# Linear attention with a gated convolution behind it: token-major products of queries with kv for the first two batches

## The chip, the cores and the metric

The kernel runs on one core of a Trainium2 chip. The metric is the device time of one execution in microseconds (us). A profiled execution gives the trace from which all durations here are read; its time differs a little from the median of the runs.

## The reference

For 8 batches and 8 heads, queries, keys and values have 576 tokens of 64 numbers. Features and attention, and then a gated feed forward on the 512 columns of all heads:

```python
proj = x @ w_phi                                  # 64 -> 128
proj = proj - max(abs(proj), axis=-1)
phi  = concat([exp(proj), exp(-proj)])            # 256 features
kv   = phi(k).T @ v                               # per batch and head, 256 x 64
z    = sum(phi(k), tokens)
x    = (phi(q) @ kv) / (phi(q) @ z + 1e-6)        # 576 x 64 per head
h    = relu(x @ w_in)                             # 512 -> 1024
c    = conv over 3 tokens of h with conv_w        # per column
out  = (h * sigmoid(c)) @ w_out                   # 1024 -> 512
```

The feed forward's weights come as float64 and are converted on the chip.

## The kernel before

**Units and groups.** A unit u = 2*batch + quad holds four heads as two pairs (pair index i). Its tokens go in five groups g: g = 0 is the last 64 tokens (both pairs in one group, n = 1), g = 1 to 4 are 256 tokens (n = 2) of two pairs in turn. `k_process` (L220) loads keys, projects them (`kp`, L185 ff.), subtracts the maximum (km L204, ks L206 on DVE), takes the exponentials `ke` on ACT (L236, L237) and multiplies them into `kv` (L251 for g = 0, L255 otherwise: weights are `ke`, 128 tokens by 128 features, f32; moving are 65 or 130 columns of v with a column of ones for the denominator). `q_process` (L300) projects queries, transposes them to features on partitions (`tp`, L320), takes exponentials (L326, `qe` or `qh`), and multiplies with kv to `nm` (L348 in f32, L356 in three fp32r terms of high and low halves): 65 rows, of which one is the denominator, and up to 256 token columns.

**Pairing.** Up to the first five groups of keys, a group's kv products are issued by `k_process` itself. Every later one hands its products over as a generator, and the nm products of the group five places earlier issue them alternately with their own (L331, L350 to L360; an nm, then one or two kv).

**Division.** ACT copies the denominator row (`dr`, L374), a DMA collects it into `den` (L377), ACT copies the numerator (`num`, L379). When two groups of a pair are there, `x_process` (L384) adds 1e-6 and takes the reciprocal on DVE (L392, L393), spreads it by four DMAs (`rr`, L397), broadcasts it with a stream shuffle (L405), multiplies (L406) and splits x into `xh` (ACT, L60) and `xl` (DVE, L65), for two halves c of the tokens.

**Feed forward.** `h_part` (L418) of batch b and half c multiplies x of all four pairs p with w_in in three fp32r terms (`hp`, L429), for eight column blocks; it needs x of every pair. Then relu, the convolution (POOL L452, DVE L457), sigmoid, gate, splits, and `op` with w_out (L488). The weights arrive in 16 chunks w0 to w15 (8 of w_in, then 8 of w_out) through two raw buffers and are converted by DVE (L96, L98, L100, L103), ACT (L97, L102, L60) and POOL (L105, L65).

**Order.** A planner (L513 to L586) steps these processes as generators with an own clock and ready times, and the instructions get priorities from the moment they were issued; each engine's order is fixed when the kernel is built. PE, DVE, ACT and POOL execute theirs strictly in that order. PSUM tiles of kp, qp, tp and nm share four buffers of a pool (`pg`, tag "g").

**Which units use f32.** NKV_F32 = 2: units 0 and 1 keep kv and the query features in f32 (`kvh` copied by ACT L282); later ones are split into high and low halves (kvf, kvh, kvl; ql on DVE L65).

Of the kernel before, what the change touches and what calls it, by code (L numbers as in the profile page):

```python
# [7 lines left out]
F32 = mybir.dt.float32  # L8
F32R = mybir.dt.float32r
# [19 lines left out]
AHEAD = 300  # L29

NQ_F32 = 2
NKV_F32 = 2


@with_exitstack
def kernel(
# [13 lines left out]
    nc = tc.nc  # L50
    cp = ctx.enter_context(tc.tile_pool(name="cp", bufs=1))
    sb = ctx.enter_context(tc.tile_pool(name="sb", bufs=1))
    pg = ctx.enter_context(tc.tile_pool(name="pg", bufs=4, space=bass.MemoryType.PSUM))
# [3 lines left out]
    def split(src, hi, lo, eng_hi, eng_lo):  # L57

        if eng_hi is nc.scalar:
            nc.scalar.activation(out=hi, in_=src, func=AF.Copy)  # L60
        elif eng_hi is nc.gpsimd:
            nc.gpsimd.tensor_scalar(out=hi, in0=src, scalar1=1.0, scalar2=0.0, op0=ALU.mult, op1=ALU.add)  # L62
        else:
            nc.vector.tensor_copy(out=hi, in_=src)
        eng_lo.tensor_tensor(out=lo, in0=src, in1=hi.bitcast(F32), op=ALU.subtract)  # L65
# [13 lines left out]
    idn = load_const(ident, [P, P], "idn")  # L79
# [73 lines left out]
    def pe(ns):  # L153
        return ("pe", ns)
# [61 lines left out]
    kv = {}  # L216
# [3 lines left out]
    def k_process(b, qd, g):  # L220
        j = (b * NQ + qd) * 5 + g
# [5 lines left out]
        n, hi, lo = load_split(kT, b, qd, g, "k")  # L227
# [6 lines left out]
        pr = project(n, hi, lo, b, qd, g, "k")  # L234
# [22 lines left out]
                                             start=False, stop=(g % 2 == 0 and t == 1), skip_group_check=True)  # L257
                        yield ins

        if j < 5:  # L260
            for _ in products():
                pass
            yield pe(860 * n)
        else:


            kvgen[j] = products()
            set_ready(("ke", j))
            yield until(("kvd", j))
        if g == 4:  # L270
# [3 lines left out]
            r = []  # L274
# [23 lines left out]
    xh, xl = {}, {}  # L298

    def q_process(b, qd, g):  # L300
        j = (b * NQ + qd) * 5 + g

        def back(key, k):
            return (key, *divmod(j - k, 5)) if j >= k else None

        yield until(back("qp", 2))
        n, hi, lo = load_split(qT, b, qd, g, "q")
# [3 lines left out]
        pr = project(n, hi, lo, b, qd, g, "q")  # L311
# [10 lines left out]
        qh = sb.tile([P, 2, 2, n * P], F32 if f32 else F32R, name=f"qh{b}_{qd}_{g}", tag="qh", bufs=2)  # L322
# [5 lines left out]
                split(e, qh[:, s], ql[:, s], nc.scalar, nc.vector)  # L328
        yield pe(220 * n)
        yield wait(3000)  # L330
        paired = j + 5 < 5 * NQ * B  # L331
        yield until(back("num", 1), ("kvq", b, qd), ("ke", j + 5) if paired else None)

        parts = [(0, 0, 512, 64), (1, 64, 512, 64)] if g == 0 else [((g - 1) // 2, 0, (g - 1) % 2 * 256, 256)]
        for pr_, _, _, _ in parts:
# [2 lines left out]
        ps = pg.tile([VW, 2, n * P], F32, name=f"nm{b}_{qd}_{g}", tag="g", bufs=4)  # L338
        ins = None
        for pr_, o, s0, w in parts:  # L340
            for i in range(2):
                khi, klo, kf = kv[b, qd][i]
                k = 0
                for s in range(2):
                    c_ = slice(pr_ * VW, (pr_ + 1) * VW)
                    a, x = (kf if f32 else khi)[:, s, c_], qh[:, s, i, o : o + w]
                    if f32:
                        ins = after(ins, lambda: nc.tensor.matmul(out=ps[:, i, o : o + w], lhsT=a, rhs=x,  # L348
                                                                  start=(s == 0), stop=(s == 1)))
# [17 lines left out]
        for pr_, o, s0, w in parts:  # L367
# [3 lines left out]
            dn, nt = den[b, qd, pr_], numt[b, qd, pr_]  # L371
# [9 lines left out]
        if g == 2 or g == 4:  # L381
            spawn(x_process(b, qd * 2 + g // 2 - 1))

    def x_process(b, p):  # L384
        yield ("wait", 4000)
        qd, pr = divmod(p, 2)
        dn, nt = den[b, qd, pr], numt[b, qd, pr]
        if 4 * b + p > 0:
            yield until(("x", *divmod(4 * b + p - 1, 4), 1))
        with tc.high_priority():  # L390
            rc = sb.tile([72, 16], F32, name=f"rc{b}_{p}", tag="rc", bufs=2)
            nc.vector.tensor_scalar(out=dn, in0=dn, scalar1=1e-6, scalar2=None, op0=ALU.add)  # L392
            nc.vector.reciprocal(out=rc, in_=dn)  # L393
            for i in range(2):
                for j in range(2):
                    row = D * i + 32 * j
                    nc.sync.dma_start(out=rr[row : row + 1, :].rearrange("o (r c) -> o r c", c=16),  # L397
                                      in_=rc.rearrange("(r i) c -> i r c", i=2)[i])
        yield ("wait", 4500)
        for c in range(2):  # L400
            yield until(("h", 2 * (b - 1) + c) if b > 0 else None)
            t0 = 0 if c == 0 else S - HW
            with tc.high_priority():
                xf = sb.tile([P, HW], F32, name=f"xf{b}_{p}_{c}", tag="xf", bufs=2)
                nc.vector.stream_shuffle(out=xf, in_=rr[:, t0 : t0 + HW], mask=[0] * 32)  # L405
                nc.vector.tensor_tensor(out=xf, in0=nt[:, t0 : t0 + HW], in1=xf, op=ALU.mult)  # L406
                xh[b, p, c] = sb.tile([P, HW], F32R, name=f"xh{b}_{p}_{c}", tag="xh", bufs=8)
                xl[b, p, c] = sb.tile([P, HW], F32R, name=f"xl{b}_{p}_{c}", tag="xl", bufs=8)
                split(xf, xh[b, p, c], xl[b, p, c], nc.scalar, nc.vector)
            set_ready(("x", b, p, c), 2500)  # L410
            yield pe(125)
# [117 lines left out]
    start = {}  # L529
# [113 lines left out]
```

## Time and profile before

| | |
|---|---|
| runs (us) | 824.35, 826.24, 827.76; median 826.24 |
| profiled execution (us) | 825.6, of which the span of the trace 823.5 |
| PE busy | 788.0 us (96%) |
| DVE busy | 645.6 us (78%) |
| ACT busy | 569.5 us (69%) |
| POOL busy | 307.6 us (37%) |

The span is from the first to the last instruction. An f32 matmul stands in the trace as two records; a PE row such as "x4" counts records. Matmuls are pipelined, so one record lasts about 0.28 us while the next can start 0.11 us after it; a price is therefore taken from starts. The granted clock (PEclk) is 1.00 at 2.4 GHz and 0.50 at 1.2 GHz.

### The profile page before, as it was taken

Reading aid. Unit: us, or ns where it says so; the run is one execution under the profiler, and the core shown is the slowest. Engines: PE = TensorE matmul, PEld = TensorE weight load, DVE = VectorE, ACT = ScalarE, POOL = GpSimd, SP = SyncE. Lnnn points to the kernel's source line nnn. Section 1 sums busy time; section 2 is a strip of 40 time slices with the busy share of each in tenths; the row PEclk is TensorE's granted clock in tenths of the full one; section 3 lists DMA queues with packets and bytes.
Section 4 is the critical chain, followed back from the end, with each engine's and each line's share of the span. In section 5 each row is a group of like instructions: output and inputs, shape, how many; then the busy total and the mean of one; then the engine's idle time right before and its main releaser. Section 6 shows DMA issues by size and latency. Waiting matters only on the chain.

```text
span 823.5 us, 17817 instructions
## 1 busy us (share of the span) xinstructions
PE 788.0 (96%) x6350; PEld 772.5 (94%) x6350; DVE 645.6 (78%) x1390; ACT 569.5 (69%) x1228; POOL 307.6 (37%) x467
## 2 busy tenths in 40 slices
PE   7778779999999999999999999999999999999998
PEld 6767678999999999999999999999999999999998
DVE  4879999799987769787779878788697878766551
ACT  4598777797788867687586857678576867644332
POOL 4757765444443424414233333424334131111110
PEclk9799989999999999999999999999999999999999
DMA  6544421211211302121121211112021100000001
GB/s 187 157 134 135 135 66 47 67 41 44 70 56 44 93 18 71 27 82 50 46 61 43 69 34 60 47 50 82 15 77 29 56 12 19 13 30 30 23 23 44
DMA packets 56328, 49.18 MB, mean 60 GB/s; under 512 B 15024, under 2 KB 54192, under 8 KB 56240
## 3 DMA queue, kind: packets, MB, share of 16 engines
q1 hardware_dynamic: 56240, 48.05, 20.1%
q8 instruction: 51, 0.84, 0.4%
q14 instruction: 37, 0.30, 0.1%
HBM read 38.13 MB, written 9.44 MB: 58 GB/s over the span
## 4 chain that ended last, share of the span: by engine, by line
PE 74%; DVE 10%; ACT 7%; issue 4%; DMA 3%; POOL 1%; SPq 1%; DVEq 0%; ACTq 0%; POOLq 0%
PE op L488 22%; PE hp L429 21%; PE kv L255 8%; PE nm L356 8%; PE tp L320 3%; PE kp L199 2%; PE nm L348 2%; PE kp L200 2%; PE kp L201 2%; PE qp L199 1%; PE qp L200 1%; PE qp L201 1%; DMA w_r<-in_w_in_dram 1%; PE kv L251 1%; DVE qm L204 1%
## 5 line engine op out<-in xcount | busy, mean ns | idle before, releaser
L457 DVE SCALAR_TENSOR_TENSOR c<-h,cw,c 128x287 f32<-128x287 f32 (+1 forms) x256 | 138.7, 554 | 49.4 <-POOL c L452 47.5
L452 POOL TENSOR_SCALAR c<-h,cw 128x288 f32<-128x288 f32 x128 | 75.0, 588 | 243.6 <-ACT h L436 184.3
L255 PE MATMUL kv<-v,ke 128*128 128x65 f32 x1024 | 159.4, 255 | 1.4 <-ACT ke L236 1.2
L255 PEld LDWEIGHTS kv<-v,ke 128*128 128x128 f32 x1024 | 153.5, 193 | 4.8 <-ACT ke L236 1.8
L429 PE MATMUL hp<-xh,win_hi 128*128 128x290 f32 x512 | 153.2, 300 | 0.6 <-ACT os L493 0.6
L429 PE MATMUL hp<-xl,win_hi 128*128 128x290 f32 x512 | 152.7, 298 | 0.2 <-DVE xl L65 0.2
L488 PE MATMUL op<-gh,wout_hi 128*128 128x288 f32 x512 | 152.2, 298 | 0.0
L429 PE MATMUL hp<-xh,win_lo 128*128 128x290 f32 x512 | 151.9, 297 | 0.0
L488 PE MATMUL op<-gl,wout_hi 128*128 128x288 f32 x512 | 151.4, 296 | 0.0
L488 PE MATMUL op<-gh,wout_lo 128*128 128x288 f32 x512 | 150.9, 295 | 0.0
L436 ACT ACTIVATE h<-hp 128x290 f32<-128x290 f32 x128 | 52.2, 414 | 71.7 <-PE hp L429 71.2
L429 PEld LDWEIGHTS hp<-xh,win_hi 128*128 128x128 f32 x512 | 96.7, 190 | 1.5 <-ACT os L493 1.4
L62 POOL TENSOR_SCALAR kxh<-kr 128x256 fp32r<-128x256 f32 (+1 forms) x80 | 43.8, 547 | 144.1 <-PE kp L200 134.6
L429 PEld LDWEIGHTS hp<-xl,win_hi 128*128 128x128 f32 x512 | 97.0, 189 | 0.6 <-DVE xl L65 0.6
L429 PEld LDWEIGHTS hp<-xh,win_lo 128*128 128x128 f32 x512 | 97.1, 190 | 0.0
L488 PEld LDWEIGHTS op<-gh,wout_lo 128*128 128x128 f32 x512 | 96.4, 188 | 0.0
L488 PEld LDWEIGHTS op<-gl,wout_hi 128*128 128x128 f32 x512 | 96.2, 188 | 0.0
L488 PEld LDWEIGHTS op<-gh,wout_hi 128*128 128x128 f32 x512 | 96.1, 188 | 0.0
L65 DVE TENSOR_TENSOR ql<-qe,qh 128x512 fp32r<-128x512 f32 x112 | 79.9, 732 | 9.9 <-ACT qh L60 9.5
L236 ACT ACTIVATE ke<-ks 128x512 f32<-128x512 f32 (+1 forms) x80 | 46.9, 586 | 39.1 <-DVE ks L206 36.5
L326 ACT ACTIVATE qe<-tp 128x512 f32<-128x512 f32 x112 | 61.2, 595 | 12.2 <-PE tp L320 10.4
L356 PE MATMUL nm<-ql,kvh 128*65 128x256 f32 x224 | 68.4, 308 | 0.3 <-DVE ql L65 0.2
(84 smaller groups left out, 1989.5 us busy)
## 6 DMA issues: line engine op xcount, KB each, us to landing
v<-in_vt_dram SPq DMA_DIRECT2D x80, 130.0 KB
out_dram<-os SPq DMA_DIRECT2D x64, 144.0 KB
qr<-in_qT_dram SPq DMA_DIRECT2D x64, 128.0 KB
kr<-in_kT_dram SPq DMA_DIRECT2D x64, 128.0 KB
w_r<-in_w_in_dram SPq DMA_DIRECT2D x8, 512.0 KB
w_r<-in_w_out_dram SPq DMA_DIRECT2D x8, 512.0 KB
rr<-rc SPq DMA_DIRECT2D x128, 2.2 KB
qr<-in_qT_dram SPq DMA_DIRECT2D x16, 64.0 KB
```

The lines of the kernel that those rows point to most:

```text
L62: nc.gpsimd.tensor_scalar(out=hi, in0=src, scalar1=1.0, scalar2=0.0, op0=ALU.mult, op1=ALU.add)
L65: eng_lo.tensor_tensor(out=lo, in0=src, in1=hi.bitcast(F32), op=ALU.subtract)
L199: nc.tensor.matmul(out=o, lhsT=his, rhs=wbd_hi, start=True, stop=False)
L236: nc.scalar.activation(out=e[:, 0], in_=pr, func=AF.Exp)
L255: ins = nc.tensor.matmul(out=kp[i][:, s, p0 : p0 + VW], lhsT=lhsT, rhs=v[:, (2 * t + i) * VW : (2 * t + i + 1) * VW], start=False, stop=(g ...
L326: nc.scalar.activation(out=e, in_=tp.rearrange("p i t s -> p i (t s)"), func=AF.Exp, scale=1.0 - 2.0 * s)
L356: ins = after(ins, lambda: nc.tensor.matmul(out=ps[:, i, o : o + w], lhsT=w_, rhs=x_, start=(k == 0), stop=(k == 5)))
L429: nc.tensor.matmul(out=ps, lhsT=w_, rhs=x_, start=(k == 0), stop=(k == 11))
L436: nc.scalar.activation(out=hs, in_=ps, func=AF.Relu)
L452: nc.gpsimd.tensor_scalar(out=cv, in0=hs[:, o : o + TC], scalar1=cw[:, f, 1:2], scalar2=0.0, op0=ALU.mult, op1=ALU.add)
L457: nc.vector.scalar_tensor_tensor(out=cv[:, lo:hi], in0=hs[:, o + j - 1 + lo : o + j - 1 + hi], scalar=cw[:, f, j : j + 1], in1=cv[:, lo:hi ...
L488: nc.tensor.matmul(out=ps, lhsT=w_, rhs=x_, start=(k == 0), stop=(k == 23))
```

## The change

For units 0 to 3 (N_TOK = 4), `q_process` calls the new `token_products` in place of nm, dr, den and num, and `x_process` is not run for these units. `nt` has tokens on partitions: the query features are the weights (128 tokens wide), kv is moving (65 columns a pair and 128 tokens; 130 for g = 0), in f32. DVE adds 1e-6 to the denominator columns (`rd`), takes the reciprocal and multiplies out of PSUM into `xt`; PE transposes xt back into the same PSUM tile; ACT and DVE split that tile directly into xh and xl, in pieces of the groups' tokens. NKV_F32 becomes 4, so units 2 and 3 keep kv and query features in f32 and have no ql, kvf, kvl any more. PAIR_FROM = 5: the kv products of units 1 to 4, up to there paired, are issued by `k_process` alone. The tiles of x are allocated (`x_tiles`) when group 0 of a unit comes to its products; for batch 1 that waits for the h parts of batch 0.

```diff
-NKV_F32 = 2
+NKV_F32 = 4
+N_TOK = 4
+PAIR_FROM = 5
...
-        if j < 5:
+        if j < 5 * PAIR_FROM:
             for _ in products():
                 pass
             yield pe(860 * n)
...
-        paired = j + 5 < 5 * NQ * B
+        paired = 5 * PAIR_FROM <= j + 5 < 5 * NQ * B
         yield until(back("num", 1), ("kvq", b, qd), ("ke", j + 5) if paired else None)
+
+        if 2 * b + qd < N_TOK:
+            yield from token_products(b, qd, g, n, qh)
+            set_ready(("num", *divmod(j, 5)))
+            return
...
+    def token_products(b, qd, g, n, qh):
+        if g == 0:
+            if b > 0:
+                yield until(("h", 2 * b - 2), ("h", 2 * b - 1))
+            for pr in range(2):
+                for c in range(2):
+                    x_tiles(b, 2 * qd + pr, c)
+            ps = pg.tile([P, 2, 2, VW], F32, name=f"nt{b}_{qd}_{g}", tag="g", bufs=4)
+            for i in range(2):
+                for s in range(2):
+                    nc.tensor.matmul(out=ps[:, i].rearrange("p r w -> p (r w)"), lhsT=qh[:, s, i, :],
+                                     rhs=kv[b, qd][i][2][:, s, :], start=(s == 0), stop=(s == 1))
+        else:
+            c_ = slice((g - 1) // 2 * VW, (g - 1) // 2 * VW + VW)
+            ps = pg.tile([P, 2, 2, VW], F32, name=f"nt{b}_{qd}_{g}", tag="g", bufs=4)
+            for t in range(2):
+                for i in range(2):
+                    for s in range(2):
+                        nc.tensor.matmul(out=ps[:, t, i, :], lhsT=qh[:, s, i, t * P : (t + 1) * P],
+                                         rhs=kv[b, qd][i][2][:, s, c_], start=(s == 0), stop=(s == 1))
+        yield pe(900 * n)
+        with tc.high_priority():
+            rd = sb.tile([P, 2, 2], F32, name=f"rd{b}_{qd}_{g}", tag="m", bufs=4)
+            nc.vector.tensor_scalar(out=rd, in0=ps[:, :, :, D], scalar1=1e-6, scalar2=None, op0=ALU.add)
+            nc.vector.reciprocal(out=rd, in_=rd)
+            xt = sb.tile([P, n, 2, D], F32, name=f"xt{b}_{qd}_{g}", tag="xf", bufs=2)
...
+                nc.vector.tensor_tensor(out=xt, in0=ps[:, :, :, 0:D],
+                                        in1=rd.unsqueeze(3).broadcast_to([P, 2, 2, D]), op=ALU.mult)
+            xp = ps.rearrange("p a b w -> p (a b w)")[:, 0 : n * P]
+            for t in range(n):
+                nc.tensor.transpose(out=xp[:, t * P : (t + 1) * P], in_=xt[:, t].rearrange("p i d -> p (i d)"),
+                                    identity=idn)
...
+            for pr, c, o, d0, w in pieces:
+                p = 2 * qd + pr
+                split(xp[:, o : o + w], xh[b, p, c][:, d0 : d0 + w], xl[b, p, c][:, d0 : d0 + w], nc.scalar, nc.vector)
+        yield pe(110 * n)
+        if g == 2 or g == 4:
+            for c in range(2):
+                set_ready(("x", b, 2 * qd + g // 2 - 1, c), 5000)
```

In the rows of order below, a name is a tile with batch, quad and group (nt0_1_4 is batch 0, quad 1, group 4; xl0_3_0 is batch 0, pair 3, half 0; w15 the last chunk of weights), and the last number is a running one. The new kernel's line numbers are 2 higher in this part (L67 for L65, L105 for L103, L257 for L255, L493 for L429).

On DVE, before, around the last part of batch 0's x, which is one split of 290 columns between the steps of w15:

```order
L206 TENSOR_TENSOR ks1_1_4_1512<-kp1_1_4_1503,km1_1_4_1510 128x512
L98 TENSOR_SCALAR w15_t_897<-w15_r_895 128x512
L100 SCALAR_TENSOR_TENSOR w15_t_897<-w15_r_895,w15_t_897 128x512
L65 TENSOR_TENSOR xl0_3_0_1527<-xf0_3_0_1523,xh0_3_0_1526 128x290
L103 SCALAR_TENSOR_TENSOR w15_t_897<-w15_t_897,w15_r_895 128x512
L65 TENSOR_TENSOR xl0_3_1_1534<-xf0_3_1_1530,xh0_3_1_1533 128x290
```

The same place on DVE in the new kernel, rows 164 to 170, where before had it at rows 181 to 186:

```order
L429 TENSOR_TENSOR xt0_1_4_1128<-nt0_1_4_1116,rd0_1_4_1125 128x256
L100 TENSOR_SCALAR w15_t_956<-w15_r_954 128x512
L102 SCALAR_TENSOR_TENSOR w15_t_956<-w15_r_954,w15_t_956 128x512
L67 TENSOR_TENSOR xl0_3_0_863<-nt0_1_3_1076,xh0_3_0_862 128x256
L105 SCALAR_TENSOR_TENSOR w15_t_956<-w15_t_956,w15_r_954 128x512
L206 TENSOR_REDUCE qm1_0_1_1154<-qp1_0_1_1147 128x4
L67 TENSOR_TENSOR xl0_3_0_863<-nt0_1_4_1116,xh0_3_0_862 128x34
```

The split has become pieces out of the PSUM tile nt, and the attention beside it is of unit 2's first query groups (qm1_0_1) instead of unit 3's last key group (ks1_1_4).

On PE, before, where the first hp products of batch 0 get the last x (rows 391 to 399):

```order
L200 MATMUL qp1_1_1_1548<-wbd_lo_73,qxh1_1_1_1419 128x256
L201 MATMUL qp1_1_1_1548<-wbd_hi_72,qxl1_1_1_1420 128x256
L429 MATMUL hp0_0_1598<-xh0_3_0_1526,win_hi3_96 128x290
L429 MATMUL hp0_1_1613<-xh0_3_0_1526,win_hi3_96 128x290
L429 MATMUL hp0_0_1598<-xl0_3_0_1527,win_hi3_96 128x290
L429 MATMUL hp0_0_1598<-xh0_3_0_1526,win_lo3_100 128x290
L429 MATMUL hp0_1_1613<-xl0_3_0_1527,win_hi3_96 128x290
L429 MATMUL hp0_1_1613<-xh0_3_0_1526,win_lo3_100 128x290
L199 MATMUL qp1_1_2_1567<-wbd_hi_72,qxh1_1_2_1425 128x256
```

The same products on PE in the new kernel, rows 283 to 293, behind a transpose of x:

```order
L322 MATMUL tp1_0_0_1198<-idn_76,qs1_0_0_1114 128x128 x2
L433 MATMUL nt0_1_4_1116<-idn_76,xt0_1_4_1128 128x128 x2
L253 MATMUL kv1_1_0_1212<-v1_1_0_1052,ke1_1_0_1144 128x130 x2
L253 MATMUL kv1_1_1_1213<-v1_1_0_1052,ke1_1_0_1144 128x130 x2
L493 MATMUL hp0_0_1268<-xh0_3_0_862,win_hi3_96 128x290
L493 MATMUL hp0_1_1283<-xh0_3_0_862,win_hi3_96 128x290
L493 MATMUL hp0_0_1268<-xl0_3_0_863,win_hi3_96 128x290
L493 MATMUL hp0_0_1268<-xh0_3_0_862,win_lo3_100 128x290
L493 MATMUL hp0_1_1283<-xl0_3_0_863,win_hi3_96 128x290
L493 MATMUL hp0_1_1283<-xh0_3_0_862,win_lo3_100 128x290
L322 MATMUL tp1_0_1_1204<-idn_76,qs1_0_1_1156 128x128
```

They stand some 105 rows earlier, at the first groups of unit 2's queries instead of unit 3's.

On PE, before, the start of a paired group of unit 2 (rows 336 to 345), nm between single kv products of unit 3:

```order
L356 MATMUL nm1_0_2_1436<-qh1_0_2_1315,kvh1_0_0_1185 65x256
L255 MATMUL kv1_1_0_1195<-v1_1_2_1151,ke1_1_2_1336 128x65
L356 MATMUL nm1_0_2_1436<-ql1_0_2_1316,kvh1_0_0_1185 65x256
L255 MATMUL kv1_1_0_1195<-v1_1_2_1151,ke1_1_2_1336 128x65
L356 MATMUL nm1_0_2_1436<-qh1_0_2_1315,kvl1_0_0_1186 65x256
L356 MATMUL nm1_0_2_1436<-qh1_0_2_1315,kvh1_0_0_1185 65x256
L255 MATMUL kv1_1_1_1196<-v1_1_2_1151,ke1_1_2_1336 128x65
```

On PE in the new kernel, products of the same units (rows 359 to 368):

```order
L415 MATMUL nt1_0_1_1610<-kvh1_0_0_1194,qh1_0_1_1209 128x65
L257 MATMUL kv1_1_0_1212<-v1_1_1_1164,ke1_1_1_1229 128x65
L257 MATMUL kv1_1_1_1213<-v1_1_1_1164,ke1_1_1_1229 128x65
L257 MATMUL kv1_1_0_1212<-v1_1_1_1164,ke1_1_1_1229 128x65
L257 MATMUL kv1_1_1_1213<-v1_1_1_1164,ke1_1_1_1229 128x65
L257 MATMUL kv1_1_0_1212<-v1_1_1_1164,ke1_1_1_1229 128x65 x2
L257 MATMUL kv1_1_0_1212<-v1_1_2_1178,ke1_1_2_1254 128x65 x4
L257 MATMUL kv1_1_1_1213<-v1_1_1_1164,ke1_1_1_1229 128x65 x2
L257 MATMUL kv1_1_1_1213<-v1_1_2_1178,ke1_1_2_1254 128x65 x4
L322 MATMUL tp1_0_2_1628<-idn_76,qs1_0_2_1241 128x128
```

The small products stand in runs of their own, with no wide product between them.

## Rows read from the trace of the kernel before

**Rows 1.** Stretches: PE, weight loads, DVE, ACT, POOL busy (count), PEclk, DMA, GB/s.

```profile
60.00:80.00 20.00, 16.96 (x125) 14.44 (x124) 19.96 (x40) 17.65 (x39) 15.97 (x18) 1.00 0.49 153
...
100.00:120.00 20.00, 13.15 (x90) 12.05 (x89) 20.00 (x37) 14.21 (x30) 12.20 (x13) 0.83 0.29 88
...
200.00:400.00 200.00, 199.79 (x1690) 199.09 (x1689) 162.39 (x360) 149.17 (x324) 73.72 (x120) 1.00 0.19 54
```

**Rows 2.** Timeline of PE, 97 to 130 us: start, us, instruction, idle before and releaser.

```profile
103.50 1.09 PE L320 MATMUL tp<-idn,qs 128*128 128x128 f32 x4 [3.41 <-DVE ks L206]
...
120.76 0.36 PE L199 MATMUL kp<-wbd_hi,kxh 128*128 128x256 f32 x1 [2.01 <-POOL wout_lo L65]
...
127.77 0.38 PE L199 MATMUL qp<-wbd_hi,qxh 128*128 128x256 f32 x1 [1.31 <-ACT qh L326]
```

**Rows 3.** Timeline of DVE, in 40 to 50 and 92 to 127 us.

```profile
42.82 0.45 DVE L98 TENSOR_SCALAR w_t<-w_r 128x512 int32<-128x512 int32 x1 [4.60 <-ACT w_t L97]
...
97.56 1.55 DVE L65 TENSOR_TENSOR xl<-xf,xh 128x290 fp32r<-128x290 f32 x1
...
100.39 0.68 DVE L204 TENSOR_REDUCE qm<-qp 128x4 f32<-128x512 f32 x1
100.99 0.41 DVE L65 TENSOR_TENSOR kvl<-kvf,kvh 128x260 fp32r<-128x260 f32 x1
...
119.40 0.41 DVE L206 TENSOR_TENSOR qs<-qp,qm 128x256 f32<-128x256 f32 x1
119.73 1.55 DVE L406 TENSOR_TENSOR xf<-num,xf 128x290 f32<-128x290 f32 x2
...
124.39 0.45 DVE L65 TENSOR_TENSOR xl<-xf,xh 128x290 fp32r<-128x290 f32 x1
```

**Rows 4.** Timeline of PE, 18 to 23 us: a run of unpaired kv.

```profile
18.94 3.24 PE L255 MATMUL kv<-v,ke 128*128 128x65 f32 x28
```

**Rows 5.** Timeline of PE, 30 to 36 us: a run of transposes and what follows.

```profile
34.09 0.60 PE L320 MATMUL tp<-idn,qs 128*128 128x128 f32 x4
34.52 0.39 PE L251 MATMUL kv<-v,ke 128*128 128x130 f32 x2
```

**Rows 6.** Timeline of PE, 57 to 61 us: first row of a paired f32 group, first behind it.

```profile
57.27 0.59 PE L348 MATMUL nm<-qh,kvh 128*65 128x256 f32 x2
...
60.57 0.28 PE L320 MATMUL tp<-idn,qs 128*128 128x128 f32 x1
```

**Rows 7.** Timeline of PE, 128 to 134 us: paired fp32r group, first rows, first behind it.

```profile
128.58 0.27 PE L356 MATMUL nm<-qh,kvh 128*65 128x256 f32 x1
128.69 0.33 PE L255 MATMUL kv<-v,ke 128*128 128x65 f32 x2
128.83 0.31 PE L356 MATMUL nm<-ql,kvh 128*65 128x256 f32 x1
...
131.38 0.30 PE L429 MATMUL hp<-xh,win_hi 128*128 128x290 f32 x1
```

**Rows 8.** Timeline of PE, 63 to 66 us: group 0 of a unit, first rows, first behind it.

```profile
63.70 0.28 PE L348 MATMUL nm<-qh,kvh 128*65 128x64 f32 x2
63.82 0.44 PE L251 MATMUL kv<-v,ke 128*128 128x130 f32 x2
64.10 0.28 PE L348 MATMUL nm<-qh,kvh 128*65 128x64 f32 x2
...
65.72 0.51 PE L429 MATMUL hp<-xh,win_hi 128*128 128x290 f32 x2
```

**Rows 9.** Groups on DVE by shape: busy us and mean ns of the weight conversions.

```profile
L103 DVE SCALAR_TENSOR_TENSOR w_t<-w_t,w_r 128x512 f32<-128x512 int32 x16 | 14.8, 922 | 0.0
L100 DVE SCALAR_TENSOR_TENSOR w_t<-w_r,w_t 128x512 int32<-128x512 int32 x16 | 12.4, 777 | 0.0
...
L98 DVE TENSOR_SCALAR w_t<-w_r 128x512 int32<-128x512 int32 x16 | 9.6, 602 | 6.5 <-ACT w_t L97 6.5
L96 DVE TENSOR_SCALAR w_t<-w_r 128x512 int32<-128x512 int32 x16 | 8.6, 539 | 2.0 <-DMA w_r<-in_w_in_dram 1.0 <-POOL wout_lo L65 0.8
```

More of the change, by code (lines that the diff above doesn't have):

```diff
@@ L382, in q_process, with x_tiles @@
             spawn(x_process(b, qd * 2 + g // 2 - 1))
+    def x_tiles(b, p, c):
+        xh[b, p, c] = sb.tile([P, HW], F32R, name=f"xh{b}_{p}_{c}", tag="xh", bufs=8)
+        xl[b, p, c] = sb.tile([P, HW], F32R, name=f"xl{b}_{p}_{c}", tag="xl", bufs=8)
+    def token_products(b, qd, g, n, qh):
[24 more added lines that the diff above has]
+            xt = sb.tile([P, n, 2, D], F32, name=f"xt{b}_{qd}_{g}", tag="xf", bufs=2)
+            if g == 0:
+                for r in range(2):
+                    h = slice(64 * r, 64 * r + 64)
+                    nc.vector.tensor_tensor(out=xt[h, 0], in0=ps[h, :, r, 0:D],
+                                            in1=rd[h, :, r].unsqueeze(2).broadcast_to([64, 2, D]), op=ALU.mult)
+            else:
+                nc.vector.tensor_tensor(out=xt, in0=ps[:, :, :, 0:D],
[4 more added lines that the diff above has]
+                                    identity=idn)
+            if g == 0:
+                pieces = [(0, 1, 0, 226, 64), (1, 1, 64, 226, 64)]
+            elif g % 2 == 1:
+                pieces = [(g // 2, 0, 0, 0, 256)]
+            else:
+                pieces = [(g // 2 - 1, 0, 0, 256, HW - 256), (g // 2 - 1, 1, S - HW - 256, 0, 512 - (S - HW))]
+            for pr, c, o, d0, w in pieces:
[5 more added lines that the diff above has]
+                set_ready(("x", b, 2 * qd + g // 2 - 1, c), 5000)
@@ L406, in x_process @@
                 nc.vector.tensor_tensor(out=xf, in0=nt[:, t0 : t0 + HW], in1=xf, op=ALU.mult)
-                xh[b, p, c] = sb.tile([P, HW], F32R, name=f"xh{b}_{p}_{c}", tag="xh", bufs=8)
-                xl[b, p, c] = sb.tile([P, HW], F32R, name=f"xl{b}_{p}_{c}", tag="xl", bufs=8)
+                x_tiles(b, p, c)
                 split(xf, xh[b, p, c], xl[b, p, c], nc.scalar, nc.vector)
```

## The prediction

> **What bounds the kernel now.** I read the busy times by stretch first. Later in the span TensorE (PE) never waits: 199.79 of 200 us busy in 200 to 400 [rows 1]. There the end moves one for one with PE's work. At the start PE is short of work: 16.96 of 20 us in 60 to 80, 13.15 in 100 to 120, where the granted clock is also 0.83, and VectorE (DVE) is the engine without a pause, 19.96 and 20.00 [rows 1]. Two things can therefore move the time: how much work PE has, and when PE stops losing time at the start.
>
> The second I read in PE's timeline. Between 100 and 128 us it stands still for 3.41 us (for ks on DVE), 2.01 (for wout_lo on POOL) and 1.31 us (for qh on ACT) [rows 2]; with three more between them (1.22 us the longest; six in all) that is 8.9 us. The clock share 0.83 of the same 20 us means that about 6.8 us ran at 1.2 instead of 2.4 GHz, after the 3.41 us stop; that is 3.4 us of work lost. Losses from 100 to 140: about 12 us. They end when the feed forward of batch 0 has its input: the last half of x, xl0_3_0, leaves DVE at 124.4 + 0.45 us [rows 3], and PE takes the hp products that wait for it right behind the wait that ends at 127.77 [rows 2]. From there PE always has a product to run.
>
> **The change, first part: PE's work.** For units 0 to 3 (batches 0 and 1) I compare a whole group g of 256 tokens.
> - Unpaired key product: a run of 28 records of `kv` lasts 3.24 us [rows 4]; less one record's own 0.28 us that is 2.96 us for 27 steps, 0.11 us a record. One f32 matmul is two records, so 0.22 us.
> - The new `nt` has the same shape (128 columns of weights, 65 moving), so I give it 0.22 us as well. Per group 8 kv + 8 nt = 3.52 us.
> - A transpose: four take 34.52 - 34.09 = 0.43 us with what follows, 0.108 each [rows 5]. Two per group: 0.22. After: 3.74 us.
> - Before, units 0 and 1: four nm and eight kv in turns, 57.27 to 60.57 = 3.30 us [rows 6]. Units 2 and 3: twelve nm and eight kv in turns, 128.58 to 131.38 = 2.80 us [rows 7]. There the small kv matmuls hide beside the wide nm; unpaired they do not.
> - Difference: 8 groups x 0.44 + 8 groups x 0.94 = 11.0 us. In the new order 16 of these 256 small matmuls stand right behind a projection or an hp product, which hides about 0.08 us each (in rows 7's stretch two records beside an nm cost 0.14 where they cost 0.22 in a run): -1.3 us.
> - Group 0 (64 tokens) of each unit: 63.70 to 65.72 = 2.02 us before [rows 8]; after, four kv and four nt of 130 columns at 0.22 to 0.28 each (the pair of records there is followed 0.28 us later [rows 8]) and a transpose: 1.9 to 2.35 us. Even, or +0.3 four times; +0.3 in sum taken.
>
> Sum +10 us; bounds 8.5 (more hiding beside wide products) and 12.5 (no hiding, dear group 0). The 36 transposes rest on a pitch in a run; the ones that stand alone could cost their whole latency, but they are followed by independent matmuls in most places. The Trainium skill (TensorE: Matmul & The Clock Gate, Part 4: PE-mode transpose) gives about 275 ns for a transpose in a kernel's context; as a price per transpose that would make the sum 6 us larger and the time about 830. The run of four above stands against it as a price.
>
> **Second part: when batch 0's feed forward can start.** Before, x goes through den and rr by DMA and through shuffle, mult and split on DVE. In the new order all of that is gone for batches 0 and 1, and xl0_3_0 stands at DVE's row 170 instead of 184, with less attention ahead of it. The sum on DVE from w4's L98, at 42.82 us now [rows 3] and in nearly the same row of both orders:
> - weights w4 to w15: 12 x (0.602 + 0.777 + 0.922) + 11 x 0.539 = 33.5 us [rows 9]; starts lie closer than durations (about 0.07 us, as in the 512-wide reductions below), so about 30.5.
> - attention: 23 operations of 512 columns at 100.99 - 100.39 = 0.60, 8 of 256 columns at 119.73 - 119.40 = 0.33 [rows 3]: 16.4 us.
> - tokens, not in the trace: 18 small (rd, reciprocal), 8 xt of 256 columns and two half ones, 15 xl pieces. Nearest are the 256-wide operations that read PSUM, 0.33 us, less for narrow ones; small ones taken at half of that. About 9.5 us. Upper bound: the xl of the kernel before reads two SBUF operands, and one took 1.55 us at 97.56, with POOL busy beside it, where another took 0.45 at 124.39 [rows 3]; at 1.2 us more each the 15 xl cost 18 us more. Lower bound: 7 us.
>
> 42.8 + 30.5 + 16.4 + 9.5 = 99.2, and 2 to 4 us of DVE waiting, as DVE had none to speak of in 60 to 80 and 100 to 120 [rows 1], but the new loop has more steps: about 102 us, where before had 124.8. I take the low price for xl, since the rows that read PSUM in the crowded stretch keep their length (qm at 100.39, qs at 119.40).
> The Trainium skill (SBUF — State Buffer, Who interferes with whom) says that a DVE instruction with two SBUF inputs is held up by a GpSimd instruction reading SBUF, and one with at most one such input is not. The new xt and xl have one input in PSUM, so by it the 18 us are excluded; the two lengths of xl above agree with the rule, no row here shows a split out of PSUM.
>
> ACT and POOL do not take over: ACT has 17.65, POOL 15.97 us in 60 to 80 [rows 1], and ACT loses the num and dr copies of these units and gets only the xh split back. SP loses six den and eight rr transfers per unit from its queue; no row here has PE waiting for those, so it costs nothing. What the new wait holds up: the transposes L433 stand in PE's row behind xt on DVE; behind them PE's projections wait, and for those DVE. Up to 102 us that loop has slack on PE (3 us in 20), and I cost it in the 2 to 4 us.
>
> **The sum.** PE loses about as much up to 102 us as it does now; the 12 us after that go. Profiled execution 825.6 us (span 823.5 and 2.1 outside; the median of the runs, 826.2, is 0.6 above): 825.6 + 10 - 12 = 823.6. With the bounds of PE's work 822 to 826, with a start at 98 or 106 four us to either side. So the change buys an earlier start with more products, and about breaks even. A measurement of this kernel can tell 0.5% from no change: 822.1 and 830.4.
>
> **The rivals.**
> - *Slower: the token loop starves PE.* nt (PE), rd and xt (DVE), transpose (PE), xh (ACT), xl (DVE), nine times a unit, each a place in a full DVE queue behind weight conversions, and each holding one of four PSUM buffers that projections need. One extra DVE operation (0.9 us, L103) per round in unit 1 is 8 us; batch 0 starts at 110, and the time is 831.6. It decides from 109 us on. For it: DVE has no pause and PE already stops 3.41 us for it [rows 2]. Against: DVE has 14 rows fewer to go.
> - *Faster: the early products are free.* PE has 3 of 20 us to spare while units 0 and 1 run; their 8 x 0.44 = 3.5 us then cost nothing, and batch 0 starts 4 us earlier still, at 98, since DVE's 2 to 4 us of waiting go too: 823.6 - 3.5 = 820, both together 816. Against: PE's idle time is waiting for one queue, not room at any place.
> - *It does not move the start.* The w chunks are loaded by two buffers, and the hp products need all of w_in as well as x; were the weights late, only +10 would stay: 835.6. Against: w_in is converted long before (w15, the last chunk of all, stands at DVE's row 168).
>
> **How the numbers follow.** Forecast (start at 100 to 106, 819 to 828): 0.50, of which 0.20 below 822.1 and 0.30 within. Starved loop (829 to 836): 0.19. Free early products (812 to 820): 0.24. No earlier start (about 835.6): 0.07, with 0.05 of that above 830.4. Faster 0.44; of the starved loop 0.05 is within 0.5%, so same 0.37 and slower 0.19. Leaving out the far ends of the outer cases gives 814 to 833; the forecast's own range is 819 to 828.
>
> **What would show it.** PE's timeline after: kv and nt in runs at 0.11 us a record, no alternation in the first 25 groups of keys; transposes at 0.11. DVE's timeline: xl0_3_0's last piece near 102 us and xl, xt pieces at 0.33 us; if they last over 1 us, my price is wrong. No granted clock below 1.00 after 110 us. PE's stops after 102 us below 2 us in sum; if the slices from 100 to 140 us still show a busy share of 7, the first rival holds. PE's total of matmuls grows by about 100 records. A time under 819 would say that PE's added work was dearer on paper than on the chip; one over 830 that the start did not move enough.

## The result, and the profile after

The change makes the kernel slower: 835.59 us median (832.0 to 836.43, four runs) against 826.24 (824.35 to 827.76); ratio 1.0107, 95% interval 1.0088 to 1.0126. Predicted were 823.6, range 814 to 833. The profiled execution after took 834.77 us, its span is 833.0. A ratio leaves out runs that lie over 1.5% above the fastest of their kernel (one here, of e5 below, 846.99 us).

First the busy times of the whole page of after, then PE's stretches; the columns are those of [rows 1].

```profile
PE 807.5 (97%) x6450; PEld 797.6 (96%) x6450; DVE 634.1 (76%) x1382; ACT 535.1 (64%) x1156; POOL 304.5 (37%) x467
```

```profile
40.00:60.00 20.00, 18.51 (x111) 17.43 (x109) 16.10 (x37) 12.94 (x28) 9.93 (x8) 0.70 0.46 146
60.00:80.00 20.00, 17.69 (x87) 16.28 (x87) 19.16 (x34) 11.01 (x22) 12.85 (x12) 0.67 0.43 138
...
100.00:120.00 20.00, 17.89 (x133) 17.30 (x132) 19.24 (x37) 11.37 (x26) 17.94 (x24) 0.91 0.21 61
120.00:140.00 20.00, 20.00 (x172) 20.00 (x172) 12.59 (x32) 10.24 (x17) 6.41 (x12) 1.00 0.15 40
...
200.00:400.00 200.00, 196.20 (x1669) 195.63 (x1668) 159.54 (x341) 149.15 (x330) 79.77 (x124) 0.99 0.20 58
```

Three things differ from [rows 1]. In 60 to 80 PE is busier but at a granted clock of 0.67, where before had 1.00. From 120 to 140 PE has no pause, earlier than before. And in 200 to 400, where before had 199.79 busy, 3.6 us are missing.

PE's timeline of after shows where the clock goes, how batch 0's feed forward starts, and the later stop:

```profile
43.47 1.95 PE L415 MATMUL nt<-kvh,qh 128*128 128x65 f32 x16
45.78 0.44 PE L433 MATMUL nt<-idn,xt 128*128 128x128 f32 x2 [0.36 <-DVE xt L429]
46.60 2.43 PE L415 MATMUL nt<-kvh,qh 128*128 128x65 f32 x16 [0.38 <-DVE qs L208]
48.82 1.16 PE L198 MATMUL qp<-wbd_f,qr 128*128 128x256 f32 x2
49.78 3.52 PE L257 MATMUL kv<-v,ke 128*128 128x65 f32 x16
...
105.47 0.38 PE L433 MATMUL nt<-idn,xt 128*128 128x128 f32 x2
105.68 1.06 PE L253 MATMUL kv<-v,ke 128*128 128x130 f32 x8
106.50 0.51 PE L493 MATMUL hp<-xh,win_hi 128*128 128x290 f32 x2
108.84 0.40 PE L493 MATMUL hp<-xl,win_hi 128*128 128x290 f32 x1 [1.83 <-DVE xl L67]
...
245.86 0.52 PE L201 MATMUL qp<-wbd_hi,qxh 128*128 128x256 f32 x1 [2.41 <-issue]
```

Sixteen records of nt last 1.95 us from 43.47 and those of kv 3.52 us from 49.78: the same form at 2.4 and at 1.2 GHz. The clock fell between, at 47.9, with PE paused only 0.36 and 0.38 us. The granted clock is 0.50 from 48 to 68, 75 to 82 and 109 to 113 us in after; in before only from 102 to 109 in that part (both have 24 to 34).

The hp products with the last x start at 106.50 and, for the last xl, at 108.84. In PE's timeline of before they stand at

```profile
125.48 0.43 PE L429 MATMUL hp<-xh,win_hi 128*128 128x290 f32 x2
125.75 0.30 PE L429 MATMUL hp<-xl,win_hi 128*128 128x290 f32 x1
```

and the row at 127.77 [rows 2] is a query projection behind them. So batch 0 does start 19 us earlier, and 17 us for xl. DVE's timeline of after, where [rows 3] has the split at 124.39:

```profile
104.47 1.56 DVE L100 TENSOR_SCALAR w_t<-w_r 128x512 int32<-128x512 int32 x1
105.95 1.21 DVE L102 SCALAR_TENSOR_TENSOR w_t<-w_r,w_t 128x512 int32<-128x512 int32 x1
107.08 0.41 DVE L67 TENSOR_TENSOR xl<-nt,xh 128x256 fp32r<-128x256 f32 x1
107.42 0.67 DVE L105 SCALAR_TENSOR_TENSOR w_t<-w_t,w_r 128x512 f32<-128x512 int32 x1
...
108.62 0.17 DVE L67 TENSOR_TENSOR xl<-nt,xh 128x34 fp32r<-128x34 f32 x1
```

**An account of PE.** To see where the time went I priced every record of a kernel's PE order with the mean step from start to start that the trace of before has for it and its neighbours at the full clock. The sum is PE's work; what a trace takes beyond it is lost time (waits and half clock together). Kernels with the same instructions in another order come out some 3 us apart (before 766.6, e13 below 763.3). That is the account's own error, for work and for lost time, and a smaller difference between two kernels is not shown by it.

| us | before | after |
|---|---|---|
| PE's work | 766.6 | 776.0 |
| first hp with the last x | 125.5 | 106.5 |
| work done by then | 82.5 | 68.1 |
| lost until 140 us | 45.5 | 42.0 |
| lost behind 140 us | 7.8 | 11.4 |
| lost in all | 53.3 | 53.4 |

By this account the whole difference is PE's added work, 9.4 us (8.7 with medians in place of means). The lost time, of which 12 us were to go, is the same within the error.

### The profile page after: what moved, and what is told of

Same layout as the page of the kernel before. It is cut to its first block, busy times and chain, and to the rows that moved or that the text cites. A ratio compares the mean times of both kernels' runs of the same rounds, so it can differ in the third digit from the quotient of the medians.

```text
span 833.0 us, 17834 instructions
## 1 busy us (share of the span) xinstructions
PE 807.5 (97%) x6450; PEld 797.6 (96%) x6450; DVE 634.1 (76%) x1382; ACT 535.1 (64%) x1156; POOL 304.5 (37%) x467
## 4 chain that ended last, share of the span: by engine, by line
PE 82%; DVE 7%; ACT 6%; issue 3%; DMA 2%; SPq 0%; POOL 0%; ACTq 0%; POOLq 0%; DVEq 0%
PE hp L493 23%; PE op L552 21%; PE kv L257 10%; PE nm L363 7%; PE tp L322 3%; PE nt L415 3%; PE kp L201 2%; PE kp L203 2%; PE kp L202 2%; PE qp L201 2%; PE qp L202 2%; PE qp L203 2%; PE kv L253 2%; PE nm L355 1%; DMA w_r<-in_w_in_dram 1%
## 5 line engine op out<-in xcount | busy, mean ns | idle before, releaser
L257 PE MATMUL kv<-v,ke 128*128 128x65 f32 x1024 | 157.9, 264 | 1.9 <-ACT ke L238 1.9
L493 PE MATMUL hp<-xl,win_hi 128*128 128x290 f32 x512 | 153.6, 300 | 1.9 <-DVE xl L67 1.8
L493 PE MATMUL hp<-xh,win_hi 128*128 128x290 f32 x512 | 153.9, 302 | 1.0 <-ACT os L557 0.9
L257 PEld LDWEIGHTS kv<-v,ke 128*128 128x128 f32 x1024 | 150.7, 199 | 2.8 <-ACT ke L238 2.6
L493 PE MATMUL hp<-xh,win_lo 128*128 128x290 f32 x512 | 152.7, 298 | 0.0
L64 POOL TENSOR_SCALAR kxh<-kr 128x256 fp32r<-128x256 f32 (+1 forms) x80 | 39.0, 487 | 171.1 <-PE kp L202 161.9
L493 PEld LDWEIGHTS hp<-xl,win_hi 128*128 128x128 f32 x512 | 97.3, 190 | 2.4 <-DVE xl L67 2.3
L493 PEld LDWEIGHTS hp<-xh,win_hi 128*128 128x128 f32 x512 | 96.9, 190 | 2.2 <-ACT os L557 1.9
L493 PEld LDWEIGHTS hp<-xh,win_lo 128*128 128x128 f32 x512 | 97.4, 190 | 0.1
L67 DVE TENSOR_TENSOR ql<-qe,qh 128x512 fp32r<-128x512 f32 x96 | 66.5, 710 | 18.5 <-ACT qh L62 18.0
L206 DVE TENSOR_REDUCE km<-kp 128x4 f32<-128x512 f32 (+1 forms) x80 | 50.1, 628 | 29.1 <-PE kp L203 29.0
L238 ACT ACTIVATE ke<-ks 128x512 f32<-128x512 f32 (+1 forms) x80 | 46.9, 587 | 34.5 <-DVE ks L208 31.6
L529 DVE TENSOR_TENSOR c<-c,h 128x288 f32<-128x288 f32 x128 | 54.4, 488 | 15.3 <-ACT c L525 15.3
```

The lines of the kernel that those rows point to most:

```text
L206: nc.vector.tensor_reduce(out=m, in_=ps3, axis=AX, op=ALU.max, apply_absolute_value=True)
L238: nc.scalar.activation(out=e[:, 0], in_=pr, func=AF.Exp)
L257: ins = nc.tensor.matmul(out=kp[i][:, s, p0 : p0 + VW], lhsT=lhsT, rhs=v[:, (2 * t + i) * VW : (2 * t + i + 1) * VW], start=False, stop=(g ...
L493: nc.tensor.matmul(out=ps, lhsT=w_, rhs=x_, start=(k == 0), stop=(k == 11))
L529: nc.vector.tensor_tensor(out=c4[:, f, :], in0=c4[:, f, :], in1=hs[:, o : o + TC], op=ALU.mult)
```

## The experiments

All ran beside the kernel before on one chip for each group (medians of before 826.0 to 827.2). The expectations name theories by letters. Each expectation spells out its own: A blames the granted clock, B does not and in most names DVE's queue; C and D are about what happens behind the start of batch 0's feed forward. Starts, half clock and lost time are read from the one profiled execution of a kernel.

**e1: does a run of narrow products pull the clock down?** Runs of independent products stand behind the last output of the kernel before.

```diff
+    runs(160, 256, F32, 0)
+    runs(300, 65, F32, 1)
+    runs(160, 256, F32, 2)
+    runs(300, 128, F32, 3)
+    runs(320, 256, F32R, 4)
+    runs(600, 64, F32R, 5)
+    runs(320, 256, F32R, 6)
...
```

> The kernel before with runs of independent products put behind its last output (the output is unchanged): 160 f32 products 128x256, 300 f32 128x65, 160 f32 128x256, 300 f32 128x128, 320 fp32r 128x256, 600 fp32r 128x64, 320 fp32r 128x256, then ten times 8 f32 128x65 and 8 fp32r 128x256. Every run is bound by PE alone and has no waits. Theory A (runs of narrow products pull the granted clock down while PE never waits): PEclk 1.00 in the 256-column runs, 0.50 in the run of 300 f32 128x65 once it is under way, whose record pitch goes from 0.11 to 0.21 us, so that run takes about 120 us instead of 66. Theory B (the clock falls only behind idle time): 1.00 in all runs, 66 us for the 300.

Windows inside the run of 300 f32 128x65 and inside the run of 600 fp32r 128x64 (PE busy, PEclk, DMA share, GB/s):

```profile
940.00:950.00 10.00, 10.00 (x92) 1.00 0.01 2
...
1160.00:1170.00 10.00, 10.00 (x49) 0.50 0.00 0
1240.00:1250.00 10.00, 10.00 (x49) 0.50 0.00 0
```

The f32 run that I had named stayed at 2.4 GHz, 92 records in 10 us. The narrow fp32r run, also without a wait, ran at 1.2 GHz for the last 116 of its 122 us, and came back in the 256-column run behind it. So the clock did fall without idle time in this one execution, but nt's form alone does not do it, and both theories miss something.

**e2: token products for batch 0 only.**

```diff
-NKV_F32 = 4
-N_TOK = 4
-PAIR_FROM = 5
+NKV_F32 = 2
+N_TOK = 2
+PAIR_FROM = 3
```

> The changed kernel with token products for batch 0 only (N_TOK = 2, NKV_F32 = 2, PAIR_FROM = 3). The first 100 us should look like the changed kernel's. Both theories: PE's work is 4 to 5 us above before instead of 9.4. Theory A (narrow runs, clock): half clock again between 47 and 82 us, start of batch 0's feed forward near 109, total 826 to 830. Theory B (the token loop on DVE sets the start): start near 109 also, but PE's clock does not matter; same total.

841.23 us, ratio 1.0171 (1.0144 to 1.0199): slower than the whole change, though PE's work is 767.2, 9 us less. Half clock and start (107.2) are as in after. Lost are 67.9 us, 21.6 of them behind 140 us. Neither theory had that: both said 826 to 830.

**e3: only the unpairing.**

```diff
-        if j < 5:
+        if j < 25:
...
-        paired = j + 5 < 5 * NQ * B
+        paired = 25 <= j + 5 < 5 * NQ * B
```

> The kernel before with one part of the change alone: kv products of units 1 to 4 unpaired, no token products. By pitches: units 0 and 1 +0.2 us per group, units 2 and 3 12 x 0.117 + 1.76 - 2.80 = +0.36 us per group: +4.5 us in all, 830. Theory A adds clock loss where kv runs stand with little wide work beside them (granted clock 0.5 for some 10 us or more between 40 and 100), up to 836. Theory B: no new clock loss, 830.

847.24 us, ratio 1.0244 (1.0222 to 1.0266). This is beyond both theories (830, up to 836). PE's work is 767.1 by the account, against 766.6: taking the small kv from between the wide nm costs little work, and my estimate of 4.5 us is not borne out. The 20 us are lost time: 27.7 us are lost behind 140 us, where before loses 7.8. The last unpaired run of kv starts at 177.6 us; of the lost time some 18 us lie behind 180, where the products are before's in another order. PE's two longest waits from 300 us on (what it waited for, us in total, times, longest us), both for ACT:

```profile
PE kp L199 <- ACT qe L326: 2.7, 3, 0.9
PE nm L356 <- ACT qh L60: 2.3, 1, 2.3
```

**e5, e11: w_out later in the changed kernel.** The conversions of the last eight (e11: four) chunks of weights wait for the last split of batch 0's x. The first two of these chunks are still loaded ahead of it, into the two raw buffers (in e5 from 53.8 us on).

```diff
...
+            if n == 8:
+                yield until(*[("x", 0, p, c) for p in range(4) for c in range(2)])
+            if n < 8:
+                load_weight(n)
+            else:
+                with tc.issue_after(lastx[0].ins):
+                    load_weight(n)
```

> The changed kernel with the eight chunks of w_out loaded and converted only behind the last split of batch 0's x: some 22 us of DVE work no longer stand ahead of it. Theory A (PE at half clock sets the start): the start of batch 0's feed forward moves from 109 to 100 to 105 us at most, half clock as before, time 830 to 836. Theory B (DVE's queue sets the start): start at 90 to 94 us, time 820 to 826.

> The changed kernel with only the last four chunks of w_out behind the last split of batch 0's x: 11 us of DVE work less ahead of it. Theory B: start at 100 to 103 instead of 109. Total 826 to 832 if the weights now come in time and the start's gain is kept (C), 833 to 840 if not (D).

e5: 834.2 us (median of 831.91 to 837.93), ratio 1.0088 (1.0055 to 1.0122); start 98.5, between the two theories' 100 to 105 and 90 to 94. The profiled execution took 832.76 at a mean granted clock of 0.987; the other three had 0.973 to 0.981, so it is the one with the least half clock. Its stretches:

```profile
40.00:60.00 20.00, 17.39 (x136) 15.70 (x135) 17.47 (x40) 13.38 (x29) 10.63 (x10) 1.00 0.42 135
60.00:80.00 20.00, 17.60 (x125) 16.85 (x126) 9.63 (x22) 7.71 (x18) 7.85 (x14) 0.91 0.30 90
80.00:100.00 20.00, 17.73 (x142) 17.63 (x142) 12.35 (x34) 9.96 (x24) 6.14 (x11) 0.91 0.20 52
120.00:140.00 20.00, 15.64 (x125) 14.79 (x124) 19.48 (x34) 15.42 (x28) 13.23 (x16) 1.00 0.32 99
```

DVE is half empty from 60 on, the clock hardly falls, and the start comes 8 us earlier than after's. But in 120 to 140 PE is short again, 15.64 of 20, while DVE does the conversions that were put off. Lost until 140: 35.1, behind it 17.0. e5's PE order is that of after up to about 58 us, so its timeline there can be held against the rows of after above:

```profile
43.65 1.95 PE L416 MATMUL nt<-kvh,qh 128*128 128x65 f32 x16
45.86 0.44 PE L434 MATMUL nt<-idn,xt 128*128 128x128 f32 x2 [0.26 <-DVE xt L430]
46.68 1.97 PE L416 MATMUL nt<-kvh,qh 128*128 128x65 f32 x16 [0.38 <-DVE qs L208]
48.49 0.65 PE L198 MATMUL qp<-wbd_f,qr 128*128 128x256 f32 x2
49.01 2.07 PE L257 MATMUL kv<-v,ke 128*128 128x65 f32 x16
```

The same products with the same pauses within 0.1 us, and the clock did not fall: the kv run takes 2.07 us instead of 3.52. The same order can go either way here. e11: 833.74 us, ratio 1.0092 (1.0066 to 1.0117), start 107.5 and not 100 to 103: PE was the late one although DVE had 11 us less to do. It had 20 us of half clock between 62 and 94, and it stood still once for longer than after ever does between 40 and 110 us (1.83):

```profile
66.73 2.04 PE L198 MATMUL qp<-wbd_f,qr 128*128 128x256 f32 x4 [3.67 <-issue]
```

**e7: more wide work for the clock.**

```diff
+            if b == 0:
+                wide = ps.rearrange("p a b w -> p (a b w)")[:, 0:256]
+                for _ in range(8):
+                    nc.tensor.matmul(out=wide, lhsT=wbd_hi[:, 0:P], rhs=wbd_hi, start=True, stop=True)
```

> The changed kernel with eight wide fp32r products (128x256, into the PSUM tile that nt overwrites) ahead of the nt products of each whole group of batch 0: 64 products, 7.4 us of PE work at the full clock, meant to raise PE's activity between 38 and 105 us. If the half clock of 47 to 83 us sets the start (theory A): clock 1.00 there, start of batch 0's feed forward at 100 to 104, total 828 to 834. If DVE's queue sets it (theory B): clock 1.00 there as well, but the start stays at 107 to 110 and the total at 834 to 838. If the clock falls all the same, the run tells nothing on this.

835.60 us, ratio 1.0106 (1.0082 to 1.013): the same as after, with 64 products more (6.6 us by the account). Half clock until 140 us went from 41 to 20 us, and 48 to 58 us ran at 1.00. The start did not come earlier: 111.5. PE's timeline of e7 has a stop that after does not have, and DVE's has the last piece of xl0_3_0 at 109.84:

```profile
71.17 1.50 PE L198 MATMUL qp<-wbd_f,qr 128*128 128x256 f32 x4 [4.53 <-issue]
109.84 0.20 DVE L67 TENSOR_TENSOR xl<-nt,xh 128x34 fp32r<-128x34 f32 x1 [0.56 <-ACT xh L62]
```

The split is 1.2 us later than after had it. For the stops of e7 and e11 the profile names no releaser. By the times, PE goes on 0.10 us behind DVE's ks, which reads a projection out of one of the four shared PSUM buffers (it ends at 71.07 and at 66.63), and DVE has weight conversions of 1.2 to 1.8 us just ahead of it. The added products also delay nt by up to 0.9 us a group, so this is no clean removal of the clock's part. It shows that lifting half of the half clock in this way did not bring the start, and that the added products cost nothing in sum; what they cost and what the clock gave back can't be told apart.

**e8, e9, e10: the same instructions in another order.** e8 is the changed kernel with one sigmoid planned later, e9 the kernel before and e10 the changed kernel with another latency factor in the planner.

```diff
-        yield wait(2000)
+        yield wait(12000 if n == 2 else 2000)
...
-LAT = 1.7
+LAT = 1.75
...
-LAT = 1.7
+LAT = 1.6
```

> The changed kernel with the sigmoid of the third half batch (n = 2) planned 10 us later, so that ACT does the query exponentials qe2_1_2 ahead of it instead of behind it. Theory C (the start's gain was given back in single collisions of the fixed order): PE's 2.4 us stop at 243 us and the half clock behind it vanish, 4 us less, 831 to 832. Theory D (the give-back is a shortage that turns up elsewhere): the stop moves to another place and the time stays at 835.

> The kernel before, with the planner's latency factor 1.75 in place of 1.70: the same instructions, in another order on the engines. Theory C (the fixed order behind the first 140 us decides several us): 830 to 845, with the loss in stops of PE spread over the whole span. Theory D (with PE bound, the order matters little): 825 to 829.

> The changed kernel with the latency factor 1.60: the same instructions in another order. Theory C: off 835 by 4 us or more in either direction, as its start gain is kept or lost later. Theory D: 833 to 837.

e8: 842.92 us, ratio 1.0195 (1.0163 to 1.0227). The stop at 243 us is gone, but others came: lost behind 140 us 20.3 instead of 11.4, and the time is neither theory's. e9: 832.39 us, ratio 1.007 (1.0046 to 1.0095): 5 to 6 us for order alone, all of it behind 140 us (16.5 lost instead of 7.8, of which some 3 are the account's error). e10: 836.37 us, ratio 1.0118 (1.0094 to 1.0142), 14.1 lost behind 140 us; its time is after's within 1 us, as theory D had it. So another order cost 5 to 7 us twice and nothing clear once. Each has its own stops, and the one stop that was mended did not bring its time back.

**e6, e13: w_out later in the kernel before** (all eight chunks, the last four; the edit is that of e5).

> The kernel before with all eight chunks of w_out loaded and converted behind the last split of batch 0's x; no other change, PE's work the same 767 us. If DVE's queue sets the start of batch 0's feed forward in the kernel before as well (theory B), the start goes from 125 to 100 to 110 us. If an earlier start is worth its time (theory C), the total falls by 5 us or more; if what is gained is given back while w_out is awaited and the order behind is another (theory D), it stays at 825 to 840, as the changed kernel with the same edit did at 835.6.

> The kernel before with the last four chunks of w_out behind the last split of batch 0's x. Theory B: start near 115 instead of 125. Total 818 to 824 if the gain is kept (C), 825 to 840 if not (D).

e6: 840.07 us, ratio 1.0161 (1.0132 to 1.0191); e13: 831.32, ratio 1.0062 (1.0043 to 1.0081). The starts come at 108.6 and 110.7, 17 and 15 us earlier; until 140 us 10 and 7.5 us are gained. Behind it 34.1 and 24.6 us are lost (e13's by some 3 us too many, as its work comes out 3.3 too small). Theory D in both.

**e12: only units 2 and 3 in f32.**

```diff
-NKV_F32 = 2
+NKV_F32 = 4
```

> The kernel before with one part of the change alone: NKV_F32 = 4, so units 2 and 3 have f32 kv and query features (four f32 nm instead of twelve fp32r per group, no ql, kvf, kvl). By rows: 3.30 against 2.80 us a group, 8 groups, +4 us of PE work; DVE loses 11 us of ql, part of it ahead of batch 0's x, so the start comes 3 to 6 us earlier. Total 824 to 830 with the order as good as before's, more with a worse one.

826.65 us, ratio 1.0001 (0.9986 to 1.0015). Work +3.1, start 115.6 (10 us earlier, and not 3 to 6), 3.9 us less lost until 140, 3.3 more behind it. It is the one edit with an equal time.

| | time | PE's work | start | half clock to 140 | lost to 140 | lost behind |
|---|---|---|---|---|---|---|
| before | 826.2 | 766.6 | 125.5 | 17 | 45.5 | 7.8 |
| after | 835.6 | 776.0 | 106.5 | 41 | 42.0 | 11.4 |
| e7 | 835.6 | 782.6 | 111.5 | 20 | 34.9 | 11.8 |
| e5 | 834.2 | 775.2 | 98.5 | 17 | 35.1 | 17.0 |
| e11 | 833.7 | 774.8 | 107.5 | 31 | 39.3 | 16.6 |
| e12 | 826.7 | 769.7 | 115.6 | 24 | 41.6 | 11.1 |
| e13 | 831.3 | 763.3 | 110.7 | 17 | 38.0 | 24.6 |
| e3 | 847.2 | 767.1 | 122.5 | 24 | 46.9 | 27.7 |

The time is the median of the runs, the rest is of the profiled execution, which took up to 2.5 us more or less (832.76 in e5, 836.19 in e11).

## Why the prediction was wrong

**Right: PE's added work.** Forecast +10, bounds 8.5 to 12.5; the account gives +9.4. In after 16 records of nt or kv at the full clock last as forecast (1.95 us, 0.11 a step), and two transposes at 105.47 are followed 0.21 us later, so they cost 0.105 each and not their latency. The parts were split wrongly, though: I gave 8 x 0.94 to units 2 and 3 in part for unpairing, and by the account e3 has +0.5 us for unpairing everything.

**Right: the token steps on DVE.** xl pieces last 0.41 and 0.17 us, beside POOL's work too; the high price of 1.55 us never came. The Trainium skill's rule on two SBUF inputs (SBUF — State Buffer, Who interferes with whom) fits these splits out of PSUM.

**Wrong: the price of the weight conversions.** The DVE sum was 30.5 (weights) + 16.4 + 9.5 us and 2 to 4 of waiting. In after the steps from w4's L100 at 40.86 to the split at 108.62 are 37.1 + 16.5 + 8.6, and 5.7 of waiting. I took the conversions' mean over the trace of before [rows 9] and shortened it. That mean holds in the same part of before (groups on DVE by shape, 42.8 to 124.9 us, 33.0 us in sum):

```profile
L103 DVE SCALAR_TENSOR_TENSOR w_t<-w_t,w_r 128x512 f32<-128x512 int32 x12 | 10.3, 862 | 0.0
L100 DVE SCALAR_TENSOR_TENSOR w_t<-w_r,w_t 128x512 int32<-128x512 int32 x12 | 9.0, 748 | 0.0
L98 DVE TENSOR_SCALAR w_t<-w_r 128x512 int32<-128x512 int32 x12 | 7.7, 643 | 6.5 <-ACT w_t L97 6.5
L96 DVE TENSOR_SCALAR w_t<-w_r 128x512 int32<-128x512 int32 x11 | 6.0, 541 | 0.8 <-POOL wout_lo L65 0.8
```

In after, 40.8 to 108.8 us, the same steps last 40.5 us:

```profile
L105 DVE SCALAR_TENSOR_TENSOR w_t<-w_t,w_r 128x512 f32<-128x512 int32 x12 | 11.7, 973 | 0.0
L102 DVE SCALAR_TENSOR_TENSOR w_t<-w_r,w_t 128x512 int32<-128x512 int32 x12 | 10.5, 877 | 0.0
L98 DVE TENSOR_SCALAR w_t<-w_r 128x512 int32<-128x512 int32 x11 | 10.1, 914 | 0.3 <-DMA w_r<-in_w_in_dram 0.3
L100 DVE TENSOR_SCALAR w_t<-w_r 128x512 int32<-128x512 int32 x12 | 8.2, 687 | 4.8 <-ACT w_t L99 4.7
```

Of the 47, 32 have POOL's work beside them for over 30% of their length and last 0.99 us on the mean, the other 15 last 0.59. In before it is 31 beside POOL's work at 0.79 us and 16 at 0.53. Twelve of the 47 last over 1.2 us in after, all of them beside POOL, and two in before. So as many stand beside POOL as before, and there they last longer; why is not shown. The sum allowed for POOL's work in the price of xl and not in that of the conversions. The start came at 106.5 to 109, not 102. That is the mis-sized term.

**Wrong: "PE loses about as much up to 102 us as it does now".** Before has lost 32 us when its stop of 3.41 us begins at 100; after has lost 38.4 by 106.5. It waits less but runs 24 us more at half clock until 140, which is up to 12 us of work not done (an estimate: half the pace for 24 us).

The runs speak against a full clock giving all of that back. The mean granted clock of a run tells how long it ran at 1.2 GHz: the four runs of after have 0.971 to 0.984, or 48 to 27 us, and the run at 0.971 took 836.41, that at 0.984 832.00. Among before's 37 runs beside the experiments, 31 us of half clock (0.981) go with 827.5 to 829.4 and 13 us (0.992) with 824.9 to 825.9. So 10 us of half clock go together with 1.5 to 2 us of time, and at a like clock (0.983 to 0.985; before 824.5 to 829.3) after's 832.0 is still some 5 us slower.

Neither the clock nor DVE is shown to set the start by itself: e7 lifted half of the one and e11 a good part of the other, and the starts were 111.5 and 107.5, each with a stop of PE of its own; in e5, where both were lighter, it came at 98.5. With what was still lost behind the start, 42.0 us were gone by 140, where my sum had 33.5: 8.5 of the 12 us of error.

**Wrong: nothing is lost behind the start but what before loses there.** Before loses 7.8 us behind 140 us, after 11.4: the 2.41 us stop at 243 us, which PE spends behind ACT, and half of the 3.4 us of half clock behind it. The timeline of ACT has a sigmoid with a table load on either side ahead of the query exponentials that free the buffer for PE's next projection:

```profile
239.94 1.28 ACT L525 ACT_TABLE_LOAD   x1
241.23 2.13 ACT L525 ACTIVATE c<-c 128x2304 f32<-128x2304 f32 x1
243.38 1.28 ACT L328 ACT_TABLE_LOAD   x1
244.68 1.09 ACT L328 ACTIVATE qe<-tp 128x512 f32<-128x512 f32 x2
```

That is the other 3.6 us of error, by an account good to some 3 us (that the buffer is that one is read from the times; the profile names no releaser). No other kernel that ran lost less than 11 there by the account, with or without the change, so the kernel before is the best of thirteen by this, and a change of its front should expect some loss there. That 7.8 is the least is what the runs show; that it comes from tuning is not shown.

**Misread: where batch 0's products stand in before.** The prediction has PE take them behind the wait that ends at 127.77. They stand at 125.48 to 126.46, ahead of it. So 1.31 of the 8.9 us of stops lay behind the start, and PE did not yet have a product at all times from there on. Of the signs of the prediction, the granted clock of 1.00 from 110 us on did not come either: after has 0.50 up to 113 and from 246 to 249 us.

**The rivals.** The rival "It does not move the start" gave 835.6, the measured time, but not by its mechanism: the start moved by 19 us. "The token loop starves PE" had a start at 110 and 831.6, which is nearest to what happened, though the queue's delay came from the conversions' price and not from the tokens. "The early products are free" was half true at most: in e7 6.6 us of work ahead of the start cost nothing in sum, with 21 us less of half clock.

**What stays open:** what brings the clock down at 47.9 us in after and not in e5; why the conversions last longer; and how much of the start is the clock's.

## What to carry to other kernels

Where one engine is bound to the end and starved at the start, count the work that is left when the starving ends: bringing that point forward by 19 us gained nothing here, since 14 us of work had not been done by then and 9 us were new. A price from the trace of before holds for what stood beside the operation there: the same 47 conversions took 33.0 us in before and 40.5 in after, so give such a price a range where another engine's work slows it. And in a kernel whose engines follow a fixed order, an edit at the front reorders all that is behind it. Give that a term of its own, and measure it with an edit that changes only the order: here 5 to 7 us twice and nothing clear once, and 3 to 26 us more lost behind 140 us in the twelve kernels that were not before, some of which also move or add work.

## What the runs showed of the hardware that I had not expected

PE's granted clock fell to 1.2 GHz with PE busy: for 116 us in a run of fp32r products with 64 columns that never waited (e1, one execution), and for 20 us in after with only two pauses of under 0.4 us in the 13 us before it. An f32 run with 65 columns, 600 records, stayed at 2.4 GHz for its whole 67 us. At 1.2 GHz a record of 65 columns takes 0.213 us from start to start instead of 0.112, so these runs slow down with the clock nearly in full. They do not get faster with fewer columns: 600 f32 records of 128 columns take 67 us in e1 as well.
